# An attention + expert-MLP kernel: experts' units dealt out evenly over a batch, weights prepared one chunk at a time, their second parts formed on TensorE

## The chip, the cores and the metric

The kernel runs on one core of a Trainium2 chip. The metric is the device time of one execution in microseconds. Five engines work side by side and wait for each other through semaphores: TensorE (PE in the profile, its weight loads PEld), VectorE (DVE), ScalarE (ACT), GpSimd (POOL) and SyncE (SP). In this kernel SP issues every DMA, in the order in which the program lists them.

## The reference

Attention with a threshold, over 8 batches of 8 heads with 576 positions of 64 values, and then a two-layer expert MLP on the concatenated heads.

```python
scores = scale * np.matmul(q, k.transpose(0, 1, 3, 2))
thresh = np.max(scores, axis=-1, keepdims=True) - tau
scores = np.where(scores >= thresh, scores, -1000000000.0)
scores = scores - np.max(scores, axis=-1, keepdims=True)
attn = np.exp(scores)
attn = attn / (np.sum(attn, axis=-1, keepdims=True) + 1e-09)
attn_out = np.matmul(attn, v)                     # (8, 8, 576, 64)
x = attn_out.transpose(0, 2, 1, 3).reshape(4608, 512)
h = x @ w_in                                      # (512, 2048)
g = h * (1.0 / (1.0 + np.exp(-h)))
out = g @ w_out                                   # (2048, 512)
```

## The kernel before

**Steps.** Attention runs in steps. A step is one tile of 128 query positions for a pair of heads; the last tile of a pair (`i == 4`) has 64 positions of both heads in one tile. Five steps make a *visit* (one pair of heads, nine units of the planner's clock `u`: two per step, one for `i == 4`), four visits a batch. In step `k` PE has the scores in PSUM (line 411, four products of high and low parts, one PSUM tile `s` only), DVE takes the row maximum (L424), ACT the exponential (L436), and DVE masks and sums (L454, `soft2`). The scores of step `k+1` write the same PSUM tile, so PE waits there for `soft2(k)`. In step `k+1` ACT and POOL split the weights of step `k` into two fp16 parts `hl` (L516, L522), and SP turns them with two transposing DMAs into `wT` (L544; L540 for `i == 4`). `hl` has two buffers. Two steps after a group of rows is done its product with V runs on PE (`av`, L559), which needs the `wT` of all its steps.

**Experts' units.** Batch `b`'s MLP is cut into 64 units: for each of two column ranges (256 and 320 columns) 16 `h_unit` (L606, 12 matmuls, then tanh, a product and a split into two fp16 parts by ACT and DVE, L614, L615, L626, L632) and 16 `o_unit` (L647, 12 matmuls). A range becomes `ready` when its attention is done, so batch `b`'s units run beside the attention of batch `b+1`. The loop at the end of the function deals them out: each step adds `rate * (nxt - t)` to a credit, and takes one unit from `units` for each whole credit. `rate` is set when a range becomes ready, to the units in hand divided by the time to the next range's `ready` entry (times `RATE`). The second range is ready only three steps after the first: the first range's 32 units are put into those three steps, and the second range's 32 into the rest of the batch.

**The beginning.** The weights come as 32 chunks of 128 x 512 doubles. `decode_weights` turns a chunk into fp32: POOL (L176), DVE twice (L181, L184), ACT for the sign (L189); a part left for later (`flush_signs`) lets PE form column sums of the upper bits for a scale (L199) and POOL multiply by the sign (L205). `split_weights` makes a high fp16 part on ACT (L218) and the low one on DVE (L219). `W_PLAN` places these by the planner's clock, all behind `soft2` of a step. Batch 0 has eight *low* steps (exact fp32 scores, PE transposes L361 and ACT copies L367, L368 in place of transposing DMAs), a gap of twelve units without attention (`GAP`), then twelve *high* steps; batches 1 to 7 have 20 steps each.

Of the kernel before, what the change touches and what calls it, by code (L numbers as in the profile page):

```python
# [19 lines left out]
P = 128  # L20
# [6 lines left out]
WID = 320  # L27
# [20 lines left out]
def attention_moe(  # L48
# [89 lines left out]
    make_identity(nc, ident)  # L138
    wsc = {}

# [28 lines left out]
    def decode_weights(i):  # L169
# [18 lines left out]
        sg = stage.tile([P, 512], F16, tag="wsg", name=f"wsg_{i}", bufs=2)  # L188
# [24 lines left out]
    def split_weights(i):  # L213
# [5 lines left out]
        nc.vector.scalar_tensor_tensor(  # L219
            out=w16[:, i, 512:1024], in0=w, scalar=sc, in1=hi, op0=ALU.mult, op1=ALU.subtract  # L220
        )
# [22 lines left out]
    def load_v(b, p):  # L244
        t = sb.tile([P, 2, 5, D], F32, tag="vraw", name=f"vraw_{b}_{p}", bufs=4)
        nc.sync.dma_start(out=t, in_=vL[b, :, 2 * p : 2 * p + 2])
        vraw[b, p] = t
# [169 lines left out]
    def soft1(t):  # L417
# [3 lines left out]
        sm = sb.tile([P, 10], F32, tag="small", name=f"sm_{t}", bufs=4)  # L421
# [19 lines left out]
    def soft2(t):  # L441
# [49 lines left out]
    def load_rows(v, g):  # L491
        c0, n = RANGES[g]
        _, d = rdram[v]
        R = wst[:, NW + g, :WID]
# [167 lines left out]
    def moe_units(b, c0, n):  # L662
        for f in range(NF):
            yield lambda f=f: h_unit(b, c0, n, f)
        for d in range(DM // P):
            for quarter in range(4):
                yield lambda d=d, quarter=quarter: o_unit(b, c0, n, d, quarter)
# [22 lines left out]
    def gap(n):  # L690
        nonlocal u
        for _ in range(n):
            steps.append(None)
            begin.append(u)
            u += 1

    for v, (b, p, kind) in enumerate(visits):
        if kind == "high" and p == 0:
            gap(GAP)
            first_high = u  # L700
        if b == 1 and p == 0:
            gap(GAP1)
        own = VISITS[kind]
        start.setdefault((b, p), u)
        (at if v in direct or kind == "low" else fetch_at)(u - LOAD, lambda v=v: load_qk(v))
        if kind == "low":
# [3 lines left out]
            at(u - 2, lambda v=v: scale_direct(v))  # L710
        else:
            at(u - 3, lambda v=v: split_k(v))
            at(u - 2, lambda v=v: split_q(v))
# [18 lines left out]
    for b in range(B):  # L732
        u = start[b, 0]
        for p in range(NPAIR):
            if b == 0:
                at(-4, lambda p=p: load_v(0, p))
                at(0, lambda p=p: vmax(0, p))
                at(first_high + 5 * p - 2, lambda p=p: split_v(0, p))
# [16 lines left out]
    def scale_in():  # L755
        flush_signs()
        wsc["in"] = pow2_scales(wmx[:, 0:4], "i_w")

    def scale_out():
        flush_signs()  # L760
        wsc["out"] = pow2_scales(wmx[:, 4:8], "o_w")

    for i in range(6):
        at(-2, lambda i=i: load_weights(i))
    for first, t0, t1, t2 in W_PLAN:
        for i in range(16):
# [136 lines left out]
```

## Time and profile before

| | |
|---|---|
| time, median of 2 runs | 1743.59 us (1743.39 to 1743.79) |
| the profiled execution | 1742.38 us, of which the span of the trace is 1740.6 us |
| mean granted TensorE clock | 0.87 of full speed |
| PE, PEld busy | 1287.2 us (74%), 976.2 us (56%) |
| DVE, ACT, POOL busy | 878.3 us (50%), 743.9 us (43%), 595.1 us (34%) |
| DMA | 164 MB, 70% of the 16 engines' span |

A line of the chain of waits or of the groups names engine, source line, the operation and its tiles (`out<-in`). "Idle before" is the time the engine stood still ahead of such an instruction, with what ended it. A window row gives the busy time of each engine in a stretch of the span, the clock that PE was granted there (1.00 is full speed), and the share of the 16 DMA engines. Line numbers here are those of the kernel before.

### The profile page before, as it was taken

To read this page: it belongs to the slowest core of one execution; us is meant where nothing else is said; L and a number is where in the kernel's file an instruction comes from. 1 tells how busy PE (TensorE), PEld (TensorE's weight loads), DVE (VectorE), ACT (ScalarE), POOL (GpSimd) and SP (SyncE) were. 2 spreads that over 40 slices of the span, in tenths; PEclk is the share of its full clock that TensorE was granted. 3 is DMA by queue.
4 is the path that set the end of the run, shared out by engine and by line. 5 is a ranking of instruction groups with operands and counts; after the bars stand their busy time and mean duration, and the time that the engine had idled before them with its cause. 6 is when DMAs were issued, how large, how long until landed. Compare 5 with 4: busy or idle time off the path is not lost. (4 is left out here: it accounts for less than half of the span.)

```text
span 1740.6 us, 27922 instructions
## 1 busy us (share of the span) xinstructions
PE 1287.2 (74%) x10352; PEld 976.2 (56%) x10352; DVE 878.3 (50%) x1872; ACT 743.9 (43%) x1289; POOL 595.1 (34%) x902
## 2 busy tenths in 40 slices
PE   3446772667797769867697769867796779877899
PEld 2324552445585557645585547655584557655686
DVE  5676743555345635455346536365446546454422
ACT  3353632443344535344345435344444435354332
POOL 3434242344313433334314433334313442334300
PEclk9757785788898889989899889888898889988899
DMA  7223296788948896589967995579858894778700
GB/s 226 79 84 104 64 121 84 100 101 109 98 68 107 101 108 93 75 101 114 94 77 106 100 108 94 85 97 118 93 81 104 104 106 75 93 82 111 80 13 16
DMA packets 415592, 164.28 MB, mean 94 GB/s; under 512 B 369376, under 2 KB 394464, under 8 KB 415456
## 3 DMA queue, kind: packets, MB, share of 16 engines
q1 hardware_dynamic: 415456, 162.49, 70.4%
q8 instruction: 82, 1.34, 0.4%
q14 instruction: 54, 0.44, 0.1%
HBM read 68.42 MB, written 9.58 MB: 45 GB/s over the span
## 5 line engine op out<-in xcount | busy, mean ns | idle before, releaser
L522 POOL TENSOR_TENSOR hl<-w,hl 128x288 f16<-128x288 f32 x544 | 388.2, 735 | 576.9 <-ACT hl L516 576.5
L606 PE MATMUL h<-x,wst 128*128 128x320 f16 (+1 forms) x3072 | 435.7, 304 | 26.5 <-DVE th L615 19.5
L647 PE MATMUL o<-gbuf,wst 128*128 128x320 f16 (+1 forms) x3072 | 411.1, 294 | 0.0
L454 DVE SCALAR_TENSOR_TENSOR w<-s,sm,w 128x576 f32<-128x576 f32 x288 | 225.3, 816 | 362.5 <-ACT w L436 307.0
L606 PEld LDWEIGHTS <-wst 128*128 128x128 f16 x3072 | 311.8, 104 | 137.6 <-issue 43.1
L647 PEld LDWEIGHTS <-wst 128*128 128x128 f16 x3072 | 301.3, 100 | 95.7 <-issue 13.0
L424 DVE TENSOR_REDUCE sm<-s 128x1 f32<-128x576 f32 x288 | 205.6, 751 | 197.8 <-PE s L411 197.7
L436 ACT ACTIVATE w<-s,sm 128x576 f32<-128x576 f32 x288 | 198.1, 733 | 187.6 <-DVE sm L424 184.1
L516 ACT ACTIVATE hl<-w 128x1152 f16<-128x1152 f32 (+1 forms) x152 | 160.3, 1055 | 223.8 <-DMA wT<-hl 184.4
L411 PE MATMUL s<-khi,qhi 64*128 64x288 f32 (+1 forms) x544 | 92.8, 389 | 203.0 <-DVE w L454 201.5
L559 PE MATMUL a<-wT,vhi 128*64 128x320 f16 (+1 forms) x1080 | 110.9, 342 | 135.2 <-DMA wT<-hl 134.7
L626 ACT ACTIVATE gbuf<-th 128x320 f16<-128x320 f32 (+1 forms) x252 | 111.7, 443 | 195.9 <-DVE th L615 194.2
L411 PEld LDWEIGHTS s<-khi,qhi 64*128 64x128 f32 (+1 forms) x544 | 55.1, 218 | 244.2 <-issue 230.5
L632 DVE SCALAR_TENSOR_TENSOR gbuf<-th,gbuf 128x256 f16<-128x256 f32 (+1 forms) x256 | 121.0, 472 | 104.8 <-ACT gbuf L626 102.2
L559 PEld LDWEIGHTS <-vhi 128*64 128x64 f16 x1080 | 73.8, 126 | 166.7 <-DMA wT<-hl 73.9
L615 DVE SCALAR_TENSOR_TENSOR th<-th,h 128x256 f32<-128x256 f32 (+1 forms) x256 | 115.2, 450 | 44.5 <-ACT th L614 42.4
L590 POOL TENSOR_TENSOR x<-x,x 128x320 f16<-128x320 f32 (+1 forms) x60 | 44.2, 736 | 263.1 <-ACT x L589 263.1
L614 ACT ACTIVATE th<-h,msc 128x256 f32<-128x256 f32 (+1 forms) x256 | 125.8, 491 | 17.9 <-PE h L606 11.3
L589 ACT ACTIVATE x<-x 128x320 f16<-128x320 f32 (+1 forms) x60 | 26.7, 445 | 177.7 <-DVE x L586 177.7
L427 POOL TENSOR_SCALAR sm<-sm,ntau 128x2 f32<-128x2 f32 (+1 forms) x160 | 42.8, 268 | 130.7 <-DVE sm L424 130.4
L656 ACT ACTIVATE ot<-o,msc 128x256 f32<-128x256 f32 (+1 forms) x64 | 32.0, 500 | 115.5 <-PE o L647 115.5
L411 PE MATMUL s<-khi,qlo 64*128 64x288 f32 (+1 forms) x544 | 77.7, 335 | 1.0 <-DVE qlo L341 1.0
(85 smaller groups left out, 1124.0 us busy)
## 6 DMA issues: line engine op xcount, KB each, us to landing
vraw<-in_vL SPq DMA_DIRECT2D x60, 320.0 KB
qraw<-in_qT SPq DMA_DIRECT2D x36, 320.0 KB
kraw<-in_kT SPq DMA_DIRECT2D x36, 288.0 KB
wraw<-in_w_out SPq DMA_DIRECT2D x16, 512.0 KB
wst<-rs SPq DMA_DIRECT2D x64, 80.0 KB
out_t<-ot SPq DMA_DIRECT2D x32, 160.0 KB
wT<-hl SPq DMA_TRANSPOSE x304
gbuf<-in_w_in SPq DMA_DIRECT2D x8, 512.0 KB
```

Source lines behind the costliest of these rows:

```text
L411: nc.tensor.matmul(s_ps[:, h, j, :HALF], qq[r, i * P : (i + 1) * P], kk[r, j * HALF : (j + 1) * HALF], start=(n == 0), stop=(n == len(seq) ...
L424: nc.vector.tensor_reduce(out=sm[:, h : h + 1], in_=s_ps[:, h, :, :HALF], op=ALU.max, axis=AX.XY, negate=True)
L436: nc.scalar.activation(wtile[t][:, h].rearrange("p (j c) -> p j c", j=2), sps[t][:, h, :, :HALF], AF.Exp, bias=small[t][:, h : h + 1],)
L454: nc.vector.scalar_tensor_tensor(out=w3, in0=s_ps[:, h, :, :HALF], scalar=sm[:, 2 + h : 3 + h], in1=w3, op0=ALU.is_ge, op1=ALU.mult, accum ...
L516: nc.scalar.activation(hl[:, :nh, 0:S], w[:, :nh], AF.Copy)
L522: nc.gpsimd.tensor_tensor(out=hl[:, h, S + c : S + c + HALF], in0=w[:, h, c : c + HALF], in1=hl[:, h, c : c + HALF], op=ALU.subtract,)
L559: nc.tensor.matmul(a_ps[odd * D : (odd + 1) * D, :n], vt[:, odd, kw, :], wT[v, odd, g][:, kw, :], start=(k == 0), stop=(k == len(seq) - 1),)
L606: nc.tensor.matmul(ph[:, :n], wi(c, f, lo_w), x16[b, lo_x][:, c, c0 : c0 + n], start=(k == 0), stop=(k == 11),)
L614: nc.scalar.activation(th[:, :n], ph[:, :n], AF.Tanh, scale=moe_sc[b][:, 0:1])
L615: nc.vector.scalar_tensor_tensor(out=th[:, :n], in0=th[:, :n], scalar=1.0, in1=ph[:, :n], op0=ALU.add, op1=ALU.mult,)
L632: nc.vector.scalar_tensor_tensor(out=g[:, 1, :n], in0=th[:, :n], scalar=2.0**-14, in1=g[:, 0, :n], op0=ALU.mult, op1=ALU.subtract,)
L647: nc.tensor.matmul(ps[:, :n], wo(f, d, lo_w), g[:, lo_g, :n], start=(f == 0 and k == 0), stop=(f == NF - 1 and k == 2),)
```

## The change

1. **Rate.** `rate` is now the units in hand, plus 32 for the second range while the first is dealt out, divided by the time to the *next batch's* first `ready` entry; `RATE` is gone. So the 64 units of a batch are spread over the whole of the next batch's attention.
2. **Fillers.** `W_PLAN` and the gaps are gone. The 32 decodes and 32 splits become a list of `fillers`; each step takes one to four of them, at three places: at its start, ahead of `soft2`, and behind the transposes (`FILL_LOW` and so on). They end in step 20, the first of batch 1. Until then the `o_unit`s of batch 0 wait (`late`).
3. **The low parts of the weights.** DVE's subtraction L219 is replaced by two matmuls into a PSUM bank, `diag(scale) * w` in fp32 and `-I * hi` in fp16, and an ACT copy to fp16.
4. **Order within a step of batch 0.** The scores of step `k+1` are issued right behind `soft2(k)`; the PE transposes of a low step move behind them.
5. Small: batch 0's reciprocal rows lie in tiles of their own; five buffers for `vraw`, three for `sm`, two for `sums`, one for the sign tile; loads and splits of q, k, v for batch 0 move by two or three units of the clock.

Core of the diff:

```diff
+    def weight_scale(key, c0):
+        flush_signs()
+        wsc[key] = pow2_scales(wmx[:, c0 : c0 + 4], f"{key[0]}_w")
+        wdiag[key] = const.tile([P, P], F32, name=f"wdiag_{key}", tag="vall")
+        nc.vector.tensor_scalar(
+            out=wdiag[key], in0=ident, scalar1=wsc[key][:, 0:1], scalar2=None, op0=ALU.mult
+        )
...
-        sg = stage.tile([P, 512], F16, tag="wsg", name=f"wsg_{i}", bufs=2)
+        sg = stage.tile([P, 512], F16, tag="wsg", name=f"wsg_{i}", bufs=1)
...
         nc.scalar.activation(hi, w, AF.Copy, scale=sc)
-        nc.vector.scalar_tensor_tensor(
-            out=w16[:, i, 512:1024], in0=w, scalar=sc, in1=hi, op0=ALU.mult, op1=ALU.subtract
-        )
+        rest = bank([P, 512], f"wlo_{i}", 2)
+        nc.tensor.matmul(rest, wdiag["in" if i < 4 * NK else "out"], w, start=True, stop=False)
+        nc.tensor.matmul(rest, nident, hi, start=False, stop=True)
+        nc.scalar.activation(w16[:, i, 512:1024], rest, AF.Copy)
...
-            gap(GAP)
             first_high = u
         if b == 1 and p == 0:
-            gap(GAP1)
+            first_all = len(steps)
...
+    fillers = [lambda i=i: decode_weights(i) for i in range(16)]
+    fillers += [lambda: weight_scale("in", 0), lambda: batch_scales_in(0)]
+    fillers += [lambda i=i: split_weights(i) for i in range(16)]
+    fillers += [lambda i=i: decode_weights(i) for i in range(16, 32)]
+    fillers += [lambda: weight_scale("out", 4), lambda: batch_scales(0)]
+    fillers += [lambda i=i: split_weights(i) for i in range(16, 32)]
...
-            units.extend(moe_units(b, c0, n))
-            then = [r[0] for r in ready if r[0] > k + 1]
+            units.extend(late)
+            late = []
+            units.extend(h_units(b, c0, n))
+            if fillers:
+                late = o_units(b, c0, n)
+            else:
+                units.extend(o_units(b, c0, n))
+            then = [r[0] for r in ready if r[1] > b]
             then = begin[then[0]] if then and then[0] < len(begin) else NT + 8
-            rate = len(units) / max(1, then - t)
-            rate *= RATE
+            rate = (len(units) + 32 * (c0 == 0)) / max(1, then - t)
...
+        own = FILL_LOW if t < first_high else FILL_ONE if one else FILL_HIGH
...
+        fill(own[0])
         last = live(k - 1) and steps[k - 1][0] not in direct
...
         first = work.pop(0)() if work else None
+        fill(own[1])
         if live(k):
             soft2(k)
+        soon = live(k + 1) and k < first_all - 1
+        if soon:
+            scores(k + 1)
         run_posts(first)
+        if live(k - 1) and not last:
+            soft3_direct(k - 1)
...
+        fill(own[2])
         for f in work:
             run_posts(f())
-        if live(k + 1):
+        if live(k + 1) and not soon:
             scores(k + 1)
```

What the new rate does to a step of a later batch, seen on DVE. First the program before, an ordinary step of batch 3 (its second visit's third tile): from its maximum to the next step's. `th` and `gbuf` are the two DVE operations of an `h_unit`, `w` is `soft2`.

```order
L424 TENSOR_REDUCE sm_6831<-s_6805 128x1 x2
L454 SCALAR_TENSOR_TENSOR w_80_6832,sums_6655<-s_6805,sm_6831,w_80_6832 128x576 x2
L615 SCALAR_TENSOR_TENSOR th_256_8_6871<-th_256_8_6871,h_256_8_6841 128x320
L632 SCALAR_TENSOR_TENSOR gbuf<-th_256_8_6871,gbuf 128x320
L615 SCALAR_TENSOR_TENSOR th_256_9_6893<-th_256_9_6893,h_256_9_6858 128x320
L424 TENSOR_REDUCE sm_6903<-s_6874 128x1 x2
```

And the changed program, DVE in the third tile of batch 3's first visit, again from maximum to maximum.

```order
L435 TENSOR_REDUCE sm_6165<-s_6142 128x1 x2
L465 SCALAR_TENSOR_TENSOR w_62_6166,sums_5940<-s_6142,sm_6165,w_62_6166 128x576 x2
L646 SCALAR_TENSOR_TENSOR gbuf<-th_0_7_6159,gbuf 128x256
L629 SCALAR_TENSOR_TENSOR th_0_8_6207<-th_0_8_6207,h_0_8_6175 128x256
L646 SCALAR_TENSOR_TENSOR gbuf<-th_0_8_6207,gbuf 128x256
L629 SCALAR_TENSOR_TENSOR th_0_9_6225<-th_0_9_6225,h_0_9_6194 128x256
L646 SCALAR_TENSOR_TENSOR gbuf<-th_0_9_6225,gbuf 128x256
L629 SCALAR_TENSOR_TENSOR th_0_10_6243<-th_0_10_6243,h_0_10_6210 128x256
L646 SCALAR_TENSOR_TENSOR gbuf<-th_0_10_6243,gbuf 128x256
L629 SCALAR_TENSOR_TENSOR th_0_11_6265<-th_0_11_6265,h_0_11_6228 128x256
L435 TENSOR_REDUCE sm_6277<-s_6246 128x1 x2
```

(The rows of the changed program carry its own line numbers: L435 is L424, L465 is L454, L629 and L646 are L615 and L632, L227 is L218, L232 the new copy.) An ordinary step held two units and now holds three to five. Before, 26 of the 63 units begun in batch 3's attention stand in its first two steps (13 and 13, behind 7 in the last step of batch 2); now there are 64, four or three in a step and none to two where `i == 4`. Batch 2's attention holds 84 units in place of 68, since batch 0's second range is begun later; batch 1's holds 29 in place of 33; the last step and the drain hold 64 as before (with two more or less).

What the fillers do on ACT. Before, in the low phase behind the exponential of a step, high parts (`wst<-wst,i_w_sc`) run in a row; DVE makes the low parts.

```order
L218 ACTIVATE wst<-wst,i_w_sc 128x512 x6
L189 ACTIVATE wsg_622<-wraw_527 128x512
L218 ACTIVATE wst<-wst,i_w_sc 128x512 x5
L189 ACTIVATE wsg_644<-wraw_540 128x512
L580 ACTIVATE x_0_0_444<-a_1_0_576,xscale 128x256
L507 ACTIVATE w_5_550<-w_5_550,sm_549 128x576 x2
L436 ACTIVATE w_6_658<-s_648,sm_657 128x576 x2
```

In the changed program, ACT at the first high steps: each split is a high part and a copy from PSUM (`wst<-wlo`), which waits for PE; three stand between one step's `hl` and exponential and the next step's.

```order
L232 ACTIVATE wst<-wlo_833 128x512
L530 ACTIVATE hl_837<-w_8_752 128x2x576
L447 ACTIVATE w_9_841<-s_766,sm_840 128x576 x2
L227 ACTIVATE wst<-wst,i_w_sc 128x512
L232 ACTIVATE wst<-wlo_862 128x512
L227 ACTIVATE wst<-wst,i_w_sc 128x512
L232 ACTIVATE wst<-wlo_884 128x512
L227 ACTIVATE wst<-wst,i_w_sc 128x512
L232 ACTIVATE wst<-wlo_889 128x512
L594 ACTIVATE x_0_0_433<-a_3_0_850,xscale 128x256
```

The splits moved from one or two places in the low phase and the gap into steps 6 to 10 and 16 to 20, two to four in each.

More of the change, by code (lines that the diff above doesn't have):

```diff
@@ L493, in load_rows @@
         _, d = rdram[v]
-        R = wst[:, NW + g, :WID]
+        if visits[v][0] == 0:
+            R = sb.tile([P, WID], F32, tag="wTlow", name=f"rows_{v}", bufs=2)
+        else:
+            R = wst[:, NW + g, :WID]
         for h in range(2):
@@ L660, in o_unit, with h_units, o_units @@
         return post
[L662 to L667, printed above, removed]
+    def h_units(b, c0, n):
+        return [lambda f=f: h_unit(b, c0, n, f) for f in range(NF)]
+    def o_units(b, c0, n):
+        return [
+            lambda d=d, quarter=quarter: o_unit(b, c0, n, d, quarter)
+            for d in range(DM // P)
+            for quarter in range(4)
+        ]
     visits = [(0, p, kind) for kind in ("low", "high") for p in range(NPAIR)]
@@ L688, in attention_moe @@
     u = 0
[L690 to L695, printed above, removed]
     for v, (b, p, kind) in enumerate(visits):
         if kind == "high" and p == 0:
-            gap(GAP)
             first_high = u
         if b == 1 and p == 0:
-            gap(GAP1)
+            first_all = len(steps)
         own = VISITS[kind]
         start.setdefault((b, p), u)
-        (at if v in direct or kind == "low" else fetch_at)(u - LOAD, lambda v=v: load_qk(v))
+        (at if v in direct or kind == "low" else fetch_at)(
+            u - LOAD - 2 * (kind == "high"), lambda v=v: load_qk(v)
+        )
         if kind == "low":
@@ L709, in attention_moe @@
                 at(-2, load_vlast)
-            at(u - 2, lambda v=v: scale_direct(v))
+            at(u - 4, lambda v=v: scale_direct(v))
         else:
-            at(u - 3, lambda v=v: split_k(v))
-            at(u - 2, lambda v=v: split_q(v))
+            ahead = 2 * (kind == "high")
+            at(u - 3 - ahead, lambda v=v: split_k(v))
+            at(u - 2 - ahead, lambda v=v: split_q(v))
         for i in own:
@@ L753, in attention_moe, with fill @@
             at(u - 1 if b > 1 else u + 2, lambda b=b: vscale(b))
[L755 to L761, printed above, removed]
+    fillers = [lambda i=i: decode_weights(i) for i in range(16)]
[4 more added lines that the diff above has]
+    fillers += [lambda i=i: split_weights(i) for i in range(16, 32)]
     for i in range(6):
         at(-2, lambda i=i: load_weights(i))
[L765 to L774 removed]
+    def fill(n):
+        for _ in range(min(n, len(fillers))):
+            fillers.pop(0)()
+    for b in range(1, B):
+        at(start[b, 3] + 7, lambda b=b: batch_scales(b))
     for t in sorted(k for k in todo if k < 0):
```

33 lines of the change are left out of this document (15 added, 18 removed).

## The prediction

> **What bounds the kernel now.** I read the span in stretches first, cut at the maxima with which each batch's attention begins: the low steps, the gap, the high steps, batches 1 to 7, and the drain.
>
> ```profile
> core 0: us, PE busy (x) PEld busy (x) DVE busy (x) ACT busy (x) POOL busy (x), PEclk, DMA share, GB/s
> 0.00:146.40 146.40, 65.86 (x320) 41.93 (x320) 89.54 (x166) 64.88 (x115) 53.35 (x66) 0.76 0.40 126
> 146.40:195.80 49.40, 31.18 (x207) 22.49 (x206) 35.19 (x65) 24.46 (x46) 15.67 (x18) 0.76 0.23 77
> 195.80:288.80 93.00, 59.17 (x472) 47.47 (x470) 46.91 (x91) 37.18 (x57) 42.09 (x63) 0.80 0.75 109
> 288.80:476.60 187.80, 120.28 (x910) 86.84 (x911) 88.32 (x194) 71.69 (x113) 68.53 (x107) 0.80 0.85 99
> 476.60:676.60 200.00, 159.51 (x1329) 123.03 (x1328) 102.56 (x226) 88.80 (x156) 69.03 (x108) 0.89 0.81 95
> 676.60:873.10 196.50, 148.99 (x1269) 114.52 (x1270) 98.38 (x217) 84.98 (x147) 69.36 (x109) 0.91 0.83 96
> 873.10:1064.20 191.10, 149.70 (x1293) 116.08 (x1293) 99.45 (x221) 86.49 (x150) 68.94 (x108) 0.90 0.83 99
> 1064.20:1260.10 195.90, 154.64 (x1282) 118.02 (x1281) 99.09 (x219) 85.71 (x148) 68.50 (x109) 0.89 0.76 96
> 1260.10:1450.90 190.80, 152.32 (x1289) 117.59 (x1288) 98.48 (x218) 84.76 (x148) 69.74 (x108) 0.90 0.80 99
> 1450.90:1630.60 179.70, 143.06 (x1175) 108.19 (x1174) 88.37 (x193) 79.40 (x135) 64.51 (x102) 0.89 0.74 91
> 1630.60:1740.60 110.00, 102.50 (x820) 80.01 (x818) 32.02 (x70) 35.56 (x76) 5.38 (x8) 0.96 0.16 23
> ```
>
> Batches 3 to 6 take 774 us together, 193.6 each, and PE is busy for about 151 of that; DVE, ACT and POOL are at half or below. So PE has some 45 us of idle time a batch, and nothing else is full except, at times, the DMA engines. Next, inside batch 3: how the stretch divides, and what PE waits for.
>
> ```profile
> 676.60:717.00 40.40, 39.09 (x373) 33.97 (x374) 16.47 (x40) 16.39 (x35) 6.29 (x10) 1.00 0.55 72
> 738.80:783.30 44.50, 29.28 (x237) 21.51 (x238) 25.80 (x55) 21.55 (x37) 17.11 (x27) 0.88 0.88 99
> 783.30:821.10 37.80, 29.43 (x237) 20.34 (x236) 21.51 (x46) 17.35 (x27) 17.05 (x27) 0.90 1.04 121
> PE s L411 <- DVE w L454: 29.8, 10, 5.9
> PE a L559 <- DMA wT<-hl: 16.2, 6, 8.0
> ```
>
> The first row is the two steps with 13 units each: PE is full, at clock 1.00, and the DMA engines are half idle. The next two are visits with ten units in five steps: PE busy 66% and 78%, DMA at 0.9 to 1.0. The 47.5 us of PE's idle time in this batch are 29.8 us in front of the next scores (waiting for `soft2`) and 16.2 us in front of the product with V (waiting for the transposing DMAs). Both lie in the thin steps. **The kernel alternates between a stretch bound by PE and one bound by the softmax chain and the transposes.**
>
> **The even rate, batches 3 to 7.** A step with 13 units is PE's time, so a unit taken out of it saves its PE time, here of the 256-column kind:
>
> ```profile
> L647 PE MATMUL o<-gbuf,wst 128*128 128x256 f16 x181 | 20.4, 273 | 0.0
> 1014.61 3.43 PE L647 MATMUL o<-gbuf,wst 128*128 128x320 f16 x24
> 765.39 0.85 PE L411 MATMUL s<-khi,qhi 64*128 64x288 f32 x4 [5.40 <-DVE w L454]
> 767.61 4.69 PE L606 MATMUL h<-x,wst 128*128 128x320 f16 x24
> ```
>
> 181 matmuls in 20.4 us are 1.35 us a unit; a 320-column unit is 1.72 us (24 matmuls in 3.43) and, behind a wait of 5.4 us, 2.35. At each boundary three steps hold 33 units where an even deal gives nine: 24 units move, and save 24 x 1.35 = 32 us. What they cost in the thin steps is the unknown of this prediction, *c* us each. The trace has such steps: three in place of two units in a visit's first tile. These are the maxima of the first, second and third tile of the second visits of batches 4 (three units) and 5 (two):
>
> ```profile
> 934.81 1.42 DVE L424 TENSOR_REDUCE sm<-s 128x1 f32<-128x576 f32 x2 [1.32 <-PE s L411]
> 943.00 0.75 DVE L424 TENSOR_REDUCE sm<-s 128x1 f32<-128x576 f32 x1
> 953.51 1.41 DVE L424 TENSOR_REDUCE sm<-s 128x1 f32<-128x576 f32 x2
> 1125.45 1.42 DVE L424 TENSOR_REDUCE sm<-s 128x1 f32<-128x576 f32 x2 [1.32 <-PE s L411]
> 1132.20 1.42 DVE L424 TENSOR_REDUCE sm<-s 128x1 f32<-128x576 f32 x2
> 1146.34 1.41 DVE L424 TENSOR_REDUCE sm<-s 128x1 f32<-128x576 f32 x2
> ```
>
> The step itself grows from 6.75 to 8.19 us, +1.44; but it and the next, which waits for the transposes, fall from 20.89 to 18.70. So *c* lies between -2.2 and +1.4; I take about 0, as the added time is time the transposes need anyway: 193.6 - 32 = 162 us. A second route: PE's 149 us at clock 0.91 would be 136 at 1.00; I take 142, halve the wait for the transposes (8 us) and leave 13 of the 29.8 us, for the short `i == 4` steps: 163. I use **163**: 4 x (163 - 193.6) = -122. Batch 7, which has no next batch's V to load, 179.7 to 153: -27. By *c* = +1.4 a batch stays at 195, by PE's floor with some 14 us idle it is 150.
>
> A unit behind the 5.4 us wait took 2.35 us against 1.72, and the thin visits have a clock of 0.88 to 0.90 where the full steps have 1.00. The Trainium skill ("TensorE: Matmul & The Clock Gate", Part 1) says that PE's clock halves after an idle window of about 3.4 us and is restored by as long a busy one. The trace agrees in kind; by that rule alone, with no gap that long left, the 142 would be 136 and the total some 30 us lower.
>
> **Batches 1 and 2, and the drain.** Batch 1 stays thin (29 units for 33) and its first step takes the last four splits: 187.8 to 186, -2. Batch 2 takes 16 units more: PE 159.5 + 16 x 1.6 = 185, less 6 for the warmer clock, plus 12 idle, is 191: -9. The drain begins with the same 64 units: 0.
>
> **The beginning, 288.8 us.** Its prices:
>
> ```profile
> 81.71 0.65 POOL L176 TENSOR_SCALAR wst<-wraw 128x512 f32<-128x512 f32 x1 [1.30 <-DMA wraw<-in_w_in]
> 85.10 0.64 POOL L176 TENSOR_SCALAR wst<-wraw 128x512 f32<-128x512 f32 x1 [1.63 <-DMA wraw<-in_w_out]
> 103.80 4.67 DVE L219 SCALAR_TENSOR_TENSOR wst<-wst,i_w_sc 128x512 f16<-128x512 f32 x5
> L218 ACT ACTIVATE wst<-wst,i_w_sc x16: 707/722/722, 96.5 to 119.0; 128x512 f16<-128x512 f32 x16
> L367 ACT ACTIVATE wTd<-tm 128x512 f32<-128x512 f32 x16 | 9.6, 598 | 8.8 <-PE tm L361 8.8
> 58.99 3.68 PE L377 MATMUL a<-wTd,vraw 128*64 128x256 f32 x16
> 51.97 2.29 PE L411 MATMUL s<-kraw,qraw 64*128 64x288 f32 x8
> 54.30 1.42 DVE L424 TENSOR_REDUCE sm<-s 128x1 f32<-128x576 f32 x2 [1.84 <-PE s L411]
> 58.04 0.81 DVE L454 SCALAR_TENSOR_TENSOR w<-s,sm,w 128x576 f32<-128x576 f32 x1
> ```
>
> Decodes in a row follow each other after 3.4 us in the first two rows, 1.6 of which is the wait for a chunk that overlaps the chunk before; I take 3.2. Splits follow after 0.93 us (five in 4.67). A low step without fillers is 6.9 us (51.97 to 58.85). Eight of them behind the 9.7 us of loads are 65 us, the high steps 93, and 32 x 3.2 + 32 x 0.93 = 132 for the fillers: 290, against 288.8. So today's fillers lie wholly outside the attention chain. After the change the new split is serial between ACT and PE: a high part 0.72, or as long the fp32 product on PE (16 matmuls of 256 columns, two at a time, in 3.68 us give 0.92 for 512 columns; up to 1.3 at clock 0.76), the fp16 one 0.25, the copy 0.60 (L367's): about 2.1 us, all of which ACT stands in. Serial price ahead of batch 1: 32 x 3.2 + 28 x 2.1 = 161 us. If a share *f* of it shows, the beginning is 158 + 161 *f*. Fully serial: 319. The floor is PE: 156 us busy now, less 16 units (26), plus 32 x 1.55 (50), is 180: *f* = 0.14. Decodes now stand where the chain leaves DVE alone (from 55.72, the end of the maximum, to the masking, whose second half begins at 58.04), which hides up to 2 of their 3.2 us; but in each split ACT is blocked, and the next exponential queues behind it. So I take about the middle, *f* = 0.6: 255, **-34**.
>
> One row of the decodes speaks against more interleaving:
>
> ```profile
> L181 DVE TENSOR_SCALAR wst<-wst x32: 404/1332/1373, 17.5 to 164.5; 128x512 int32<-128x512 int32 x32
> ```
>
> The same operation takes 0.40 us or 1.33. The Trainium skill ("SBUF — State Buffer", on the port pair that VectorE and GpSimd share) says that the pair is locked for a whole instruction and that the loser waits it out. By that rule the operations that today take less than the median, at most 16, would pay 0.93 us more as POOL's work now runs beside all of them: 15 us on the beginning. I leave it out of the sum.
>
> Small edits at nothing: the rows' own tiles and the loads that SP now issues two units earlier lie in a stretch where the DMA engines are at 0.2 to 0.4; without that cover a load of 0.3 MB at 100 GB/s costs 3 us. The chunks' loads are issued by the decodes and spread with them, which can only shorten the 1.3 to 1.6 us waits above. A fifth `vraw` buffer and fewer `sm` and `sums` hide nothing today. The single sign buffer makes ACT's sign wait for POOL's product of the chunk before, which is in the 3.2 us already.
>
> **Sum.** -34 - 2 - 9 - 122 - 27 = -194. The profiled execution took 1742.38 us (1.8 beyond its span, 1.2 below the median): 1548, rounded to **1550**.
>
> **Rivals.** *The transposes keep the pace.* They are the wait that takes PE's place:
>
> ```profile
> 1019.66 4.84 SPq L540 DMA_TRANSPOSE wT<-hl  x2
> 1033.86 0.43 PE L559 MATMUL a<-wT,vhi 128*64 128x320 f16 x1 [9.74 <-DMA wT<-hl]
> ```
>
> In a fourth visit 14 us pass from that issue to the product, and behind the waiting matmul stand the step's other units and the next scores in PE's queue. The thin visits of batch 3 (44.5, 37.8 and, from 821.1 to 873.1, 52.0) average 45 us at a DMA share near 1; if that is the DMA engines' own pace, a batch takes 180, batch 7 170, batch 2 its 200: -34 - 2 - 54 - 10, **1642**. Against it: the DMA share is 0.55 in the full steps, so an even deal has room. *All hidden*: *f* = 0.35 (beginning 215), batches at 156, batch 7 at 150: -74 - 2 - 9 - 150 - 30, 1477. *The change doesn't do what it says*: *c* = 1.35, units cost in thin steps what they save in full ones; only the beginning counts, near 1705, or 1740 with *f* = 0.8. *Slower*: an added unit delays the next scores by its PE time and its two DVE operations as well, because the next maximum stands behind them on DVE:
>
> ```profile
> L615 DVE SCALAR_TENSOR_TENSOR th<-th,h 128x256 f32<-128x256 f32 (+1 forms) x256 | 115.2, 450 | 44.5 <-ACT th L614 42.4
> ```
>
> *c* = 1.5 + 2 x 0.45 = 2.4 gives 24 x 1.05 x 5 = +126 and, with -36 for the beginning and batch 1, 1832; it decides from *c* = 1.65, where the loss eats the 36. The +1.44 above speaks against it.
>
> **How the numbers follow.** Chances: forecast (1500 to 1610) 0.55, transposes 0.20, all hidden 0.13, no effect 0.07, slower 0.05. The range 1465 to 1655 leaves the last two out and the tails of the others. Faster by over 2% (below 1708; 2% is about what this measurement tells from no change) 0.90, same 0.06, slower 0.04.
>
> **What would show it.** Batches 3 to 6 at 155 to 170 us, PE over 85% busy at a clock of 0.97 or more in them, the wait of the scores for `soft2` under 15 us a batch, that for the transposes under 10; DVE's first step of batch 1 at 255 us (180 to 319), with ACT waiting for PE in its copies. I am wrong if a batch stays above 180, or if the beginning passes 320.

## The result, and the profile after

The changed kernel takes 1690.02 us (median of two, 1687.43 to 1692.61), against 1743.59 before: **0.969** of it (95% interval 0.963 to 0.976). It is faster, but by 54 us where 194 were forecast, and 1690 lies outside the range of 1465 to 1655.

The stretches of the changed kernel, cut at the same maxima as those of before (low, high, batches 1 to 4 and 7, drain; batches 5 and 6 read like 4; columns as there). The profiled execution took 1687.43 us, its span is 1685.6:

```profile
core 0: us, PE busy (x) PEld busy (x) DVE busy (x) ACT busy (x) POOL busy (x), PEclk, DMA share, GB/s
0.00:131.50 131.50, 66.78 (x294) 38.24 (x295) 60.33 (x130) 53.78 (x97) 34.33 (x48) 0.82 0.38 115
131.50:308.40 176.90, 103.22 (x596) 63.31 (x595) 87.80 (x163) 83.00 (x142) 71.82 (x97) 0.75 0.52 94
308.40:477.10 168.70, 112.83 (x887) 82.83 (x888) 84.83 (x186) 72.66 (x113) 68.96 (x108) 0.85 0.93 108
477.10:675.50 198.40, 177.81 (x1511) 134.97 (x1510) 102.67 (x227) 91.12 (x161) 69.45 (x109) 0.95 0.78 99
675.50:860.40 184.90, 151.37 (x1284) 116.61 (x1282) 99.14 (x219) 85.19 (x148) 69.66 (x109) 0.91 0.80 102
860.40:1045.40 185.00, 148.60 (x1283) 114.66 (x1281) 99.43 (x220) 85.29 (x148) 69.03 (x109) 0.93 0.84 102
...
1414.50:1586.10 171.60, 143.53 (x1252) 110.54 (x1250) 92.75 (x202) 81.86 (x143) 63.77 (x101) 0.95 0.80 96
1586.10:1685.60 99.50, 96.18 (x796) 76.27 (x794) 31.06 (x70) 34.66 (x76) 5.43 (x8) 0.99 0.17 25
```

| stretch | before | forecast | after |
|---|---|---|---|
| beginning | 288.8 | 255 | 308.4 |
| batch 1 | 187.8 | 186 | 168.7 |
| batch 2 | 200.0 | 191 | 198.4 |
| batches 3 to 6, each | 193.6 | 163 | 184.8 |
| batch 7 | 179.7 | 153 | 171.6 |
| drain | 110.0 | 110 | 99.5 |

The beginning became 20 us longer. The batches gained 9 us each instead of 30. Batch 1 and the drain gained what nobody had forecast.

What engines waited for in batch 4 (860.4 to 1045.4, the stretch that the expectations below call batch 5; us in total, times, longest):

```profile
ACT hl L530 <- DMA wT<-hl: 24.1, 5, 7.3
PE a L573 <- DMA wT<-hl: 19.8, 9, 7.3
PE s L422 <- DVE w L465: 7.9, 4, 3.4
PE h L620 <- DVE th L629: 6.2, 4, 2.1
```

PE stood idle for 185.0 - 148.6 = 36.4 us; the three PE rows make up 33.9 of it. The scores' wait for `soft2` fell as forecast (under 15). The wait of the product with V for the transposes did not, and there is a new one: a fourth `h_unit` in a step waits for a PSUM bank.

One long step of the changed kernel, the second tile of the fourth visit of batch 4. Each row is start, duration, engine and operation, with the idle time before it and what ended that:

```profile
1005.84 1.42 DVE L435 TENSOR_REDUCE sm<-s 128x1 f32<-128x576 f32 x2 [3.64 <-PE s L422]
...
1008.99 1.16 ACT L530 ACTIVATE hl<-w 128x1152 f16<-128x1152 f32 x1 [7.15 <-DMA wT<-hl]
...
1010.06 1.35 ACT L447 ACTIVATE w<-s,sm 128x576 f32<-128x576 f32 x2
...
1016.49 0.45 PE L573 MATMUL a<-wT,vhi 128*64 128x320 f16 x1 [7.33 <-DMA wT<-hl]
...
1023.59 0.53 PE L422 MATMUL s<-khi,qhi 64*128 64x288 f32 x4
```

The maximum is done at 1007.3, yet the exponential starts at 1010.06. In ACT's queue `hl` of the step before stands ahead of it, and `hl` waits for one of its two buffers, which a transpose still reads. Then PE waits in the product until 1016.49, for transposes again, and the next scores stand behind that product. Two waits for the same DMAs lie one behind the other in a step of 19 us.

### The profile page after: what moved, and what is told of

Read it like the earlier page. It is cut to its first block, busy times and chain, and to the rows that moved or that the text cites. A ratio compares the mean times of both kernels' runs of the same rounds, so it can differ in the third digit from the quotient of the medians.

```text
span 1685.6 us, 28064 instructions
## 1 busy us (share of the span) xinstructions
PE 1295.1 (77%) x10448; PEld 965.4 (57%) x10448; DVE 855.9 (51%) x1843; ACT 757.2 (45%) x1321; POOL 591.7 (35%) x902
## 5 line engine op out<-in xcount | busy, mean ns | idle before, releaser
L620 PE MATMUL h<-x,wst 128*128 128x320 f16 (+1 forms) x3072 | 417.6, 294 | 49.1 <-DVE th L629 47.4
L465 DVE SCALAR_TENSOR_TENSOR w<-s,sm,w 128x576 f32<-128x576 f32 x288 | 225.2, 815 | 327.4 <-ACT w L447 260.3
L620 PEld LDWEIGHTS <-wst 128*128 128x128 f16 x3072 | 300.8, 100 | 153.0 <-issue 72.3
L661 PEld LDWEIGHTS <-wst 128*128 128x128 f16 x3072 | 302.6, 101 | 106.2 <-issue 22.9
L435 DVE TENSOR_REDUCE sm<-s 128x1 f32<-128x576 f32 x288 | 205.6, 751 | 141.5 <-PE s L422 141.4
L573 PE MATMUL a<-wT,vhi 128*64 128x320 f16 (+1 forms) x1080 | 105.6, 331 | 115.6 <-DMA wT<-hl 114.1
L422 PE MATMUL s<-khi,qhi 64*128 64x288 f32 (+1 forms) x544 | 87.6, 367 | 126.9 <-DVE w L465 125.9
L646 DVE SCALAR_TENSOR_TENSOR gbuf<-th,gbuf 128x256 f16<-128x256 f32 (+1 forms) x256 | 125.9, 492 | 95.5 <-ACT gbuf L640 92.5
L629 DVE SCALAR_TENSOR_TENSOR th<-th,h 128x256 f32<-128x256 f32 (+1 forms) x256 | 115.5, 451 | 65.6 <-ACT th L628 64.0
L422 PEld LDWEIGHTS s<-khi,qhi 64*128 64x128 f32 (+1 forms) x544 | 51.7, 203 | 168.3 <-issue 143.8
L438 POOL TENSOR_SCALAR sm<-sm,ntau 128x2 f32<-128x2 f32 (+1 forms) x160 | 42.7, 267 | 102.4 <-DVE sm L435 97.4
L422 PE MATMUL s<-khi,qlo 64*128 64x288 f32 (+1 forms) x544 | 73.3, 318 | 0.0
L422 PE MATMUL s<-klo,qlo 64*128 64x288 f32 (+1 forms) x544 | 73.1, 317 | 0.0
```

What stands on the lines that cost most here:

```text
L422: nc.tensor.matmul(s_ps[:, h, j, :HALF], qq[r, i * P : (i + 1) * P], kk[r, j * HALF : (j + 1) * HALF], start=(n == 0), stop=(n == len(seq) ...
L435: nc.vector.tensor_reduce(out=sm[:, h : h + 1], in_=s_ps[:, h, :, :HALF], op=ALU.max, axis=AX.XY, negate=True)
L465: nc.vector.scalar_tensor_tensor(out=w3, in0=s_ps[:, h, :, :HALF], scalar=sm[:, 2 + h : 3 + h], in1=w3, op0=ALU.is_ge, op1=ALU.mult, accum ...
L573: nc.tensor.matmul(a_ps[odd * D : (odd + 1) * D, :n], vt[:, odd, kw, :], wT[v, odd, g][:, kw, :], start=(k == 0), stop=(k == len(seq) - 1),)
L620: nc.tensor.matmul(ph[:, :n], wi(c, f, lo_w), x16[b, lo_x][:, c, c0 : c0 + n], start=(k == 0), stop=(k == 11),)
L629: nc.vector.scalar_tensor_tensor(out=th[:, :n], in0=th[:, :n], scalar=1.0, in1=ph[:, :n], op0=ALU.add, op1=ALU.mult,)
```

## The experiments

The runs came in five groups, and the kernel before took between 1740 and 1783 us in them, so totals are compared as ratios to the runs of the kernel before beside them. "The beginning" is the start of batch 1 in the profile. First the changed kernel once more, unchanged, as a reference.

> The changed kernel itself once more, as the reference on the chip of these runs: 0.96 to 0.975 of the kernel before; batches 3 to 6 at 184 to 189 us each, first step of batch 1 at 305 to 310.

Measured: 0.9727 (0.9688 to 0.9767), beginning 309.7, batches 3 to 6 at 189.9 to 191.7. As expected but for the batches, some 6 us longer each here.

### Which half of the change gives what

**Rate alone**, in the kernel before:

```diff
-            then = [r[0] for r in ready if r[0] > k + 1]
+            then = [r[0] for r in ready if r[1] > b]
...
-            rate = len(units) / max(1, then - t)
-            rate *= RATE
+            rate = (len(units) + 32 * (c0 == 0)) / max(1, then - t)
```

> The kernel before with the new rate rule alone. If the beginning and the rate add up: first step of batch 1 at 289 us as in the kernel before, batches 3 to 6 at 185 to 191 us as in the changed kernel, total 0.955 to 0.965 of the kernel before. If the batches need the changed beginning as well (its smaller buffers, scores ahead): batches at 191 to 196, ratio 0.985 to 1.0.

**Beginning alone**: the changed kernel with these lines turned back (0.95 for `RATE`).

> The changed kernel with the old rate rule (next ready entry, times 0.95): the new beginning alone. If the two parts add up and the batches' gain is the rate's alone: the first step of batch 1 at 305 to 311 us as in the changed kernel (308.4), batches 3 to 6 at 191 to 196 us each as in the kernel before (193.6), span 1735 to 1765. If the smaller edits that came along (three sm buffers, two of the sums, five of vraw) or the warmer start also help the batches, batches 3 to 6 at 185 to 189 and a span near 1710.

Measured: rate alone **0.9601** (0.9561 to 0.9641), beginning 288.6, batches 3 to 6 at 183.8 to 185.8, drain 99.5. Beginning alone **1.021** (1.017 to 1.025), beginning 308.5, batches 3 to 6 at 197 to 204. So the rate gives all of the batches' gain and the drain's; the new beginning alone costs about 2%, more than was expected, and batch 2 takes 219.3 us in it. In the changed kernel, too, its cost goes on behind batch 1: with the rate alone batch 2 begins at 469.0 and ends at 652.8, in the changed kernel at 477.1 and 675.5, since batch 0's units, held back until the fillers end, fill batch 2. Half of the change beats the whole.

### The batches: what took the other 22 us of each

**Product with V one step later** (S2):

```diff
-ROW_LAG, AV_LAG2 = 2, 2
+ROW_LAG, AV_LAG2 = 2, 3
```

> The changed kernel with the product with V one step later (AV_LAG2 = 3). Theory S2, PE's wait for the transposes in front of that product holds the batches (19.8 us for wT and 7.6 us for the scale's transfer in batch 5): that wait under 5 us a batch, batches 3 to 6 from 184.8 to 165 to 176 us, total 1610 to 1655. Rival S1, the step's fourth unit waits for a PSUM bank that is freed behind soft2, and S3, the two hl buffers keep ACT waiting for the same transposes (24.1 us in batch 5): the wait of PE goes, but batches stay at 180 to 186 and the total at 1665 to 1692.

Measured: 0.9434 (0.9391 to 0.9477); batches 3 to 6 at 177.4 to 178.0. Its window of batch 4, and its waits there:

```profile
851.10:1028.70 177.60, 146.71 (x1281) 112.64 (x1280) 99.72 (x218) 85.41 (x149) 69.53 (x109) 0.92 0.91 107
```

```profile
ACT hl L530 <- DMA wT<-hl: 31.9, 7, 6.2
PE h L620 <- DVE th L629: 16.8, 4, 6.3
PE s L422 <- DVE w L465: 14.1, 9, 3.3
```

PE's wait in front of the product is gone from the list. Part of it came back elsewhere: `hl` waits 31.9 us (24.1), the bank wait is 16.8 (6.2), the scores' 14.1 (7.9). S2 is right in kind; its 165 to 176 was not reached. The total gains less than the batches: the drain grew from 99.5 to 122.4 us, for a reason that is set right below.

**At most three `h_unit`s a step** (S1):

```diff
         while units and credit >= 1:
+            if any(units[0] is h for h in hs) and len(work) >= 3 and t < NT:
+                break
             work.append(units.pop(0))
```

> The changed kernel with at most three h_units dealt to one step (there are three PSUM banks for them); the rest goes on credit to the next step. Theory S1, the fourth h_unit waits for th of the first one, which stands behind soft2 on DVE, and the next scores stand behind it on PE: steps with h_units fall from 9.0 to about 7 us, PE's wait of h for th from 6.2 us in batch 5 to under 2, batches 3 to 6 from 184.8 to 170 to 178, total 1625 to 1665. Rival S2 (transposes set the pace): the short steps come to stand in front of the transposes, batches at 182 to 188, total 1675 to 1705.

Measured: 0.9535 (0.949 to 0.958); steps with three `h_unit`s 7.7 us (9.0 with four), but batches 3 to 6 at 181.3 to 187.4, and the wait for the bank in batch 4 is still 6.1 us. The two longest steps of batch 4, those with the waits for the transposes, grew instead (18.4 and 22.4 us, against 14.0 and 19.8 in the run with two sign buffers of the same group). The cap gives 1 to 2%, but as the wait for the bank stayed, that this gain is the bank's is not shown.

**`hl` behind the exponential** (S3):

```diff
-        if last:
-            soft3a(k - 1)
-            soft3p(k - 1, 0, 1)
...
         if live(k):
             soft1(k)
             soft1b(k)
         if last:
-            soft3p(k - 1, 1, 4)
+            soft3a(k - 1)
+            soft3p(k - 1, 0, 4)
```

> The changed kernel with the high part hl of step k-1 issued on ACT behind the exponential of step k instead of ahead of it. Theory S3 (hl, waiting for one of its two buffers that the transposes free, stands ahead of the exponential in ACT's queue, 24.1 us in batch 5, and so delays soft2 and the next scores): batches 3 to 6 from 185 to 172 to 180, total 1630 to 1670 where the changed kernel takes 1690. Rival S4 (the DMA engines' own time, a share of 0.84 of 185 us or about 155 us a batch, with the transposes in series behind other transfers, sets the pace): the transposes start 1.4 us later and the batches stay at 183 to 190, total 1685 to 1710.

Measured: 0.9735 (0.9686 to 0.9784), the changed kernel's own ratio; batches at 190.7 to 194.2. Its waits in batch 4:

```profile
PE a L573 <- DMA wT<-hl: 26.5, 8, 10.6
ACT hl L530 <- DMA wT<-hl: 6.4, 3, 3.1
```

Beside the unchanged kernel of the same group (27.5 us on ACT, 23.0 on PE) ACT's wait fell by 21 us and PE's grew by 3.5, to single waits of up to 10.6 us, and the batches stayed. So S3 fails as long as the product waits too: `hl`'s wait alone did not set the pace.

**Four ninths of the transposes left out** (S4 against S5), with the later product:

```diff
-                nc.sync.dma_start_transpose(out=wT[v, h, g][:, :, c : c + P], in_=hl[:, h, :])
+                nc.sync.dma_start_transpose(out=wT[v, h, g][:, 0:5, c : c + P], in_=hl[:, h, 0 : 5 * P])
```

> The changed kernel with the product one step later (AV_LAG2 = 3) and with transposes of the first five of the nine blocks of hl only: four ninths of the transposes' bytes are left out (most of the weights' low parts); the product keeps its 28 matmuls by reading five of the blocks again. Theory S4, the DMA engines' own time sets the pace of the batches (0.91 to 0.95 of 177.6 us, some 165 us a batch, in the kernel with the product one step later): DMA share under 0.75, batches 3 to 6 from 178 (or 183 on a slower chip) to 155 to 165, the waits of ACT's hl for wT from 31.9 us a batch to under 8. Rival S5, the chain of one step (maximum, exponential, masking, bank, scores) and PE's own 147 us set the pace: DMA share falls as well, but batches stay at 172 to 183.

Measured: 0.9285 (0.9239 to 0.933); batches 3 to 6 at 166.9 to 172.2. Its window of batch 4, and its waits there:

```profile
824.80:993.30 168.50, 143.34 (x1281) 111.24 (x1282) 99.99 (x218) 85.24 (x149) 69.48 (x109) 0.95 0.64 84
```

```profile
PE h L620 <- DVE th L629: 14.6, 4, 4.6
PE s L422 <- DVE w L465: 10.5, 8, 2.9
ACT hl L530 <- DMA wT<-hl: 20.2, 6, 7.2
```

DMA time fell from 0.91 x 177.6 = 162 us a batch to 0.64 x 168.5 = 108, the batch by 9 us only; by an estimate some 3 of these belong to the group, in which the kernel before took 1.4% less as well. PE's 25.2 us of idle time are now the bank (14.6) and the scores (10.5) alone, and ACT's `hl` still waits for 20.2. So both theories hold in part. By their sum the DMA engines would be a floor near 160 us, which no run reached; above it lies the order of the queues.

**Everything together, on the kernel before.** Rate and later product; then the planner's last batch set right; then `hl` behind the exponential as above.

```diff
-            then = begin[then[0]] if then and then[0] < len(begin) else NT + 8
+            then = begin[min(then[0], len(begin) - 1)] if then else NT + 8
```

> The kernel before with the new rate rule and the product one step later (AV_LAG2 = 3), nothing of the changed beginning. If the parts add up: 0.960 of the kernel before by the rate, 0.973 of that by the later product: 0.930 to 0.94; batches 3 to 6 at 176 to 181. If the later product only cured what the changed beginning's buffers did: 0.95 to 0.96.

> As the kernel before with the rate and the later product, and the planner's last batch set right: with the later product the entry of batch 7 lies behind the last step, so that batch 6's units were dealt out up to 8 units of the clock behind the end and ran in the drain. The drain from 122 to 97 to 102 us, batch 7 from 160 to 168 to 176: 8 to 14 us less than without it, 0.922 to 0.934 of the kernel before. If batch 7 grows by what the drain loses: 0.930 to 0.94.

> As the one before, with ACT's hl of step k-1 behind the exponential of step k. Theory S3 in the form that is left (once PE no longer waits for the product, hl in front of the exponential is what waits for the transposes, 31.9 us a batch): batches 3 to 6 another 4 to 10 us shorter, 0.90 to 0.92. Rival S4 (the transposes' and the other transfers' time, 0.91 to 0.95 of the batch, sets the pace): batches within 2 us of the kernel without it, or longer, as the transposes start later.

Measured: **0.9299** (0.927 to 0.9327), batches 3 to 6 at 169.8 to 180.5; **0.9189** (0.9155 to 0.9223), drain 122.5 to 103.2, batch 7 from 159.2 to 163.9; **0.9026** (0.9005 to 0.9047). Window and waits of batch 4 of the second of them, with `hl` ahead of the exponential (0.9189):

```profile
807.80:983.10 175.30, 144.59 (x1281) 112.11 (x1282) 99.73 (x218) 85.31 (x149) 69.40 (x109) 0.94 0.92 108
```

```profile
ACT hl L516 <- DMA wT<-hl: 32.0, 7, 8.6
PE h L606 <- DVE th L615: 17.2, 4, 6.9
PE s L411 <- DVE w L454: 13.1, 8, 4.3
```

The same of the third, with `hl` behind it (0.9026):

```profile
791.40:963.00 171.60, 146.03 (x1281) 112.07 (x1282) 105.16 (x218) 85.07 (x148) 74.89 (x109) 0.93 0.90 110
```

```profile
PE h L606 <- DVE th L615: 17.3, 4, 5.7
PE s L411 <- DVE w L454: 5.5, 4, 2.9
ACT hl L516 <- DMA wT<-hl: 3.4, 2, 3.1
PE a L559 <- DMA wT<-hl: 2.5, 2, 1.4
```

Alone the move of `hl` gave nothing. Behind the later product both waits for the transposes are nearly gone, 32.0 to 3.4 us on ACT and 2.5 on PE, the scores' wait falls from 13.1 to 5.5, and the ratio falls by another 1.8%. But this gain is not where S3 put it. Batches 3 to 6 fell from 174.5 to 172.5 us in the mean, 2 us each and not 4 to 10, close to the "within 2 us" of S4. Of the 14.7 us between the two spans (1596.7 and 1582.0), 8 lie in these batches and 9 in the beginning (289.7 to 280.7), whose high steps use the same transposes. The profiled execution of the last kernel was its slowest, 1583.9 us; the other four took 1570 to 1574, so no trace shows the last 10 us. What is left of PE's 25.6 us of idle time in its batch 4 is mostly the wait for the bank, 17.3 us; the cap of three `h_unit`s was not tried together with the later product.

The last kernel took 1573.8 us beside 1741.9 of the kernel before, and beats both kernels of this study by far. Its batches take 170 to 176 us with the DMA engines 0.89 to 0.98 busy.

### The beginning: six single changes, none of them the whole cause

**Two sign buffers** (T1):

```diff
-        sg = stage.tile([P, 512], F16, tag="wsg", name=f"wsg_{i}", bufs=1)
+        sg = stage.tile([P, 512], F16, tag="wsg", name=f"wsg_{i}", bufs=2)
```

> The changed kernel with two sign buffers instead of one (and four vraw buffers instead of five, to make the room). Theory T1, the one sign buffer serialises the beginning (ACT stands 70.0 us at the sign for POOL's product of the chunk before, against 23.4 in the kernel before): first step of batch 1 from 308.4 to 265 to 285 us, that wait under 30 us, total 1650 to 1668. Rivals, T2 (the splits' exchange between ACT and PE) and T3 (fillers stand ahead of the step's softmax operations): the wait goes down, but others take its place, first step of batch 1 at 300 to 309, total 1682 to 1692. Four vraw buffers: nothing.

The waits in the beginning of the changed kernel, and the first of them with two buffers:

```profile
ACT wsg L198 <- POOL wst L214: 70.0, 29, 7.2
PE s L422 <- DVE w L465: 66.5, 16, 12.1
DVE wst L190 <- POOL wst L185: 49.9, 17, 10.5
ACT wst L232 <- PE wlo L231: 29.9, 28, 4.1
```

```profile
ACT wsg L198 <- POOL wst L214: 26.1, 8, 6.2
```

Measured: 0.9645 (0.9606 to 0.9684), beginning 306.6. The largest wait of the list fell from 70.0 to 26.1 us and the beginning by 2. T1 fails: most of that wait did not lie on the path.

**Fillers all behind the transposes** (T3): `FILL_LOW, FILL_HIGH, FILL_ONE = (0, 0, 3), (0, 0, 4), (0, 0, 2)`.

> The changed kernel with all the fillers of a step behind its transposes, none ahead of the maximum or ahead of soft2. Theory T3 (fillers stand in front of the step's own operations in DVE's, ACT's and POOL's queues): first step of batch 1 from 308 to 270 to 295, total 1655 to 1680. Rival T2 (the splits' exchange between ACT and PE, wherever they stand): 300 to 312, total 1682 to 1695.

Measured: 0.9926 (0.990 to 0.9952), beginning **347.7**, 38 us longer than the reference. T3 fails with its sign reversed: the three places hide something, and one place hides less.

**Low parts on DVE** (T2): `split_weights` as in the kernel before.

> The changed kernel with the low parts of the weights formed on DVE again instead of by two matmuls and a copy. Theory T2 (in each split ACT waits for PE, 29.9 us over 28 copies, and PE for ACT, 18.1 us): first step of batch 1 from 308 to 270 to 290, total 1650 to 1675. Rival T3: 298 to 310, total 1680 to 1695, or longer, as DVE gets 32 operations of about 0.93 us more.

Measured: 0.9689 (0.9647 to 0.973), beginning 299.6. The exchange with PE costs 9 to 10 us more than DVE's 32 operations in its place, not 18 to 38.

**POOL's first operation one decode earlier** (B1), **column sums of one chunk in four** (B3):

```diff
+        if i % 16 < 15:
+            decode_first(i + 1)
...
-            for j in range(4):
+            for j in range(4 * (c == 3)):
```

> The changed kernel with POOL's first operation of a decode issued one decode earlier, so that DVE finds it done. Theory B1, a decode that stands alone in a step shows its whole chain POOL, DVE, DVE, PE, POOL, above all DVE's 49.9 us in front of the shift for POOL: first step of batch 1 from 308 to 270 to 292 and that wait under 15 us; total 16 to 38 us below the changed kernel (0.95 to 0.963 of the kernel before). Rival B2, the step's own chain (7 us of maximum, exponential, masking and, low, reciprocal and transposes) waits for other things (PE's scores behind the fillers, POOL's threshold behind POOL's products): 300 to 312, 0.965 to 0.975.

> The changed kernel with the column sums on PE formed for one chunk in four only (the scale of the weights is then found from a quarter of them, times four). Theory B3, POOL's product by the sign waits for these sums (46.0 us in the beginning) and keeps POOL's threshold and DVE's masking back: first step of batch 1 from 308 to 275 to 295, 0.95 to 0.965 of the kernel before. Rivals B1 and B2 (the sums lie beside other waits): 300 to 310, 0.968 to 0.975.

Measured: B1 0.9854 (0.9814 to 0.9893), beginning **330.1**; B3 0.9721 (0.9674 to 0.9769), beginning 304.8. What POOL waited for in the high steps of B1's kernel:

```profile
POOL wst L179 <- DMA wraw<-in_w_out: 41.0, 10, 11.3
```

The earlier operation stands in POOL's queue and waits there for a chunk that is still being loaded. The changed kernel has that wait in a smaller form, here in the step at 223.9 us:

```profile
223.47 11.83 SPq L168 DMA_DIRECT2D wraw<-in_w_out  x3
...
232.14 0.64 POOL L185 TENSOR_SCALAR wst<-wraw 128x512 f32<-128x512 f32 x1 [5.80 <-DMA wraw<-in_w_out]
...
232.81 1.37 DVE L190 TENSOR_SCALAR wst<-wst 128x512 int32<-128x512 int32 x1 [7.54 <-POOL wst L185]
...
234.82 0.81 DVE L465 SCALAR_TENSOR_TENSOR w<-s,sm,w 128x576 f32<-128x576 f32 x1
...
236.52 0.84 PE L422 MATMUL s<-khi,qhi 64*128 64x288 f32 x4 [12.14 <-DVE w L465]
```

The chunk is late, so POOL, DVE's shift, `soft2` behind it and the scores are late, in that order.

**Every second chunk of `w_out` not loaded** (B4), and the same with B1's edit:

```diff
+        if i >= 16 and i % 2:
+            wraw[i] = wraw[i - 1]
+            return
```

> The changed kernel with every second chunk of w_out not loaded (its neighbour's data is decoded in its place). Theory B4, in the high steps the chunks' loads come late (in the step at 223.9 us of the changed kernel POOL waits 5.8 us for one, DVE's shift 7.5 us for POOL, and the scores 12.1 us for soft2 behind it): first step of batch 1 from 308 to 275 to 293, all of it between 170 and 270 us of the span. Rival B2, decodes in these steps are serial without the loads: 300 to 310.

> The changed kernel with POOL's first operation issued one decode earlier and every second chunk of w_out not loaded. Alone the first made the beginning 22 us longer (POOL waited 41.0 us for the chunks' loads), the second 8 us shorter. Theory B1 with B4 (the chain of the decode is what shows, and the loads hid its cure): POOL's wait for loads under 12 us in the high steps, first step of batch 1 at 270 to 290. Rival B2 (a decode in a step costs its operations on POOL and DVE in order, whoever is early): 295 to 306.

Measured: B4 0.9632 (0.9602 to 0.9662), beginning 300.2; that step fell from 26.5 to 20.0 us, its neighbours not. With B1's edit 0.9691 (0.9664 to 0.9717), beginning 308.3: of what B1 lost, 22 us were the loads (330.1 to 308.3), and with half of them gone the earlier operation still gives nothing (300.2 to 308.3). But POOL still waits for the loads that are left, longer than the 12 us that B1's forecast asked for:

```profile
POOL wst L182 <- DMA wraw<-in_w_out: 16.3, 5, 5.6
```

So B1 found no support, and these runs do not rule it out.

**Four reliefs at once**: low parts on DVE, two sign buffers, sums of one chunk in four, half the loads of `w_out`.

> The changed kernel with four reliefs of the beginning at once: low parts on DVE, two sign buffers (and four of vraw), column sums of one chunk in four, every second chunk of w_out not loaded. Each alone moved the first step of batch 1 by -10, -2, -4 and -8 us. If they add up: 283 to 288. If each only uncovers the next (waits side by side): 255 to 280. If they are the same wait: 296 to 302.

Measured: 0.9605 (0.9565 to 0.9645), beginning **285.4**, within the 283 to 288 of "they add up". The reliefs are separate terms: about 10 for the exchange with PE, 8 for the loads, 4 and 2 for the rest. Even then the beginning is only 3 us below the 288.8 of before.

## Why the prediction was wrong, step by step

**The beginning: the share *f*.** The step that failed is "I take about the middle, *f* = 0.6". By its own formula *f* = (308.4 - 158) / 161 = 0.93. Cut at the first high step, the low part took 131.5 - 65 = 66.5 us for 16 decodes and 6 splits, priced at 63.8 (*f* = 1.04), and the high part 176.9 - 93 = 83.9 for 16 decodes and 22 splits, priced at 97.4 (0.86). So hardly anything was hidden in either. Five us of the low part lie ahead of its first maximum, which now stands behind a decode (14.8 us, 9.7 before). Half of the argument for hiding held. Rows of the changed kernel, a decode placed ahead of `soft2`:

```profile
76.94 1.37 ACT L447 ACTIVATE w<-s,sm 128x576 f32<-128x576 f32 x2 [0.35 <-DVE sm L435]
77.09 0.27 POOL L438 TENSOR_SCALAR sm<-sm,ntau 128x2 f32<-128x2 f32 x1 [2.52 <-DVE sm L435]
77.31 0.64 POOL L185 TENSOR_SCALAR wst<-wraw 128x512 f32<-128x512 f32 x1
77.92 1.15 POOL L214 TENSOR_TENSOR wst<-wst,wsg 128x512 f32<-128x512 f32 x1
77.99 1.37 DVE L190 TENSOR_SCALAR wst<-wst 128x512 int32<-128x512 int32 x1 [1.08 <-POOL wst L185]
...
79.39 0.69 DVE L193 SCALAR_TENSOR_TENSOR wst<-wraw,wst 128x512 int32<-128x512 int32 x1
...
80.00 0.81 DVE L465 SCALAR_TENSOR_TENSOR w<-s,sm,w 128x576 f32<-128x576 f32 x1
...
81.87 0.41 DVE L190 TENSOR_SCALAR wst<-wst 128x512 int32<-128x512 int32 x1
```

The exponentials end at 78.31, but `soft2` starts at 80.00. The decode's first operation, on POOL, stands behind the step's threshold (77.09), and DVE's shift starts only at 77.99. Of its 3.2 us some 1.5 are hidden, and only for the one decode in three that stands there. Five low steps with three decodes took 12.9 to 16.2 us, 15.3 in the mean, so one costs (15.3 - 6.9) / 3 = 2.8. What the three places hide together, 38 us more than one place does, the run with all fillers behind the transposes shows. The rule of the Trainium skill ("SBUF — State Buffer") that I left out of the sum stayed out rightly: the shift's median is now 656 ns where it was 1332.

```profile
L190 DVE TENSOR_SCALAR wst<-wst x32: 405/656/1370, 13.7 to 255.0; 128x512 int32<-128x512 int32 x32
```

What remains open: the runs account for some 24 us of the beginning (10 + 8 + 4 + 2), and nothing else that was tried shortened it. That the rest is the decodes' own operations in the in-order queues of DVE and POOL is argued from rows like those above, not shown by a run. No run took back the new order within a step (point 4 of the change).

**The batches: *c* and the second route.** The change saved 193.6 - 184.8 = 8.8 us a batch, so 24 x (1.35 - *c*) gives *c* = 0.98, inside the bounds of -2.2 to 1.44 but near their upper end. The step that failed is "I take about 0, as the added time is time the transposes need anyway". The second route shows where, term by term (forecast and batch 4): PE busy 142, 148.6; wait for the transposes 8, 19.8; scores 13, 7.9; bank 0, 6.2. I had counted only PE's wait for the transposes. ACT's `hl` waits for them as well, in front of the exponential, in the profile of before too; and with that wait moved away alone, PE's grew.

What the runs showed in its place is that added time is not free there: the transposes are waited for in two queues, and taking PE's wait away gave 10 us a batch (177.7 beside 187.3 with two sign buffers, the same group), taking ACT's away alone nothing. With both nearly gone, in the last kernel of the batches' runs, a batch still takes 172.5, 9 us above the forecast.

A plain sum would have warned me: the DMA share times the length of batches 3 to 6 before is 163, 159, 149 and 153 us, 156 in the mean. A batch of 163 us would have needed the DMA engines at 0.96. "The DMA share is 0.55 in the full steps, so an even deal has room" compared a share of one stretch with the whole; the sum over the batch left 7 us of room.

**The clock.** Forecast 0.97 or more in the batches; it is 0.91 to 0.95. By the rule of the Trainium skill ("TensorE: Matmul & The Clock Gate", Part 1) shorter idle windows should have restored it. The longest waits of PE in batch 4 are still 7.3 us, above the 3.4 that the page names, so the rule was not put to the test.

**Batch 1 and the drain.** Both came out better than forecast. The drain's 10.5 us belong to the rate, since the run with the rate alone has 99.5 as well: the drain holds 796 matmuls for 820, two units of 12, and PE's idle time in it fell from 7.5 to 3.3 us. Of batch 1's 19 us the rate alone gives 7 (180.4) and the new beginning alone 1 (186.8, in a group whose kernel before was 1.3% slower); why the two together give more was not tried.

**The rivals.** "The transposes keep the pace" (180 a batch, 1642 in all) was the nearest for the batches: they took 185. No rival had a beginning that grows, although my bounds allowed up to 319.

## What to carry to other kernels

Before work is dealt into thin stretches, multiply each engine's and the DMA engines' share by the length of the whole period, and compare the sums with the length you forecast. When the same DMA is waited for in two queues, take both waits away together: alone, moving `hl` gave nothing, and behind the later product it gave 1.8%. Then look where the gain lies: only 2 us of each batch were the move's. The largest entry in a list of waits need not lie on the path: cutting ACT's 70.0 us to 26.1 moved the beginning by 2.

## What the runs showed of the hardware

Leaving out four ninths of the transposes tells what they cost. The line of the DMA queue from the page of the kernel with the later product, and from that of the same with five ninths (packets, MB, share of the span):

```profile
q1 hardware_dynamic: 415456, 162.49, 74.8%
```

```profile
q1 hardware_dynamic: 276192, 126.84, 51.1%
```

The queue's time fell from 0.748 x 1666.7 = 1247 us to 0.511 x 1619.2 = 827: 420 us for 35.7 MB, or 85 GB/s over all 16 engines. The run with the rate alone, which has all the transposes and belongs to the second's group, has 0.736 x 1667.5 = 1227; by that one it is 400 us and 89 GB/s. All nine blocks would then be an estimated 900 to 945 us, about three quarters of all DMA time, for about half of the bytes; the other 82 MB would go at 250 to 270 GB/s. The Trainium skill ("DMA: Bandwidth & Descriptors", Latency and other measured facts) gives 261 GB/s as measured on one kernel for transposes with a non-contiguous middle dimension. Here it is a third of that, in packets of 256 bytes (35.7 MB in 139264 packets), and the measurement decides.

The shift L190 takes 0.41 us alone (the decode at 81.87 us, shown above) and 1.37 beside POOL's product (77.99, with the product from 77.92 to 79.07), where it ends 0.3 us behind the product. That agrees with the rule of the Trainium skill ("SBUF — State Buffer") quoted in the prediction, by which the loser waits out the whole instruction.
